# A linear-attention and GeGLU block on one core: later loads of x and Q's weights, and a down projection in pairs of row tiles

## The chip, the core and the metric

The kernel runs on one core of one Trainium2 chip. The metric is the device time in microseconds (us): 527.69 us is the median of 16 runs of the kernel before, from 526.3 to 528.41. The profile is of one execution of it, which took 526.3 us; its span, from the first to the last recorded instruction, is 524.6 us, and the remaining 1.7 us lie around it.

A core has five instruction streams that run beside each other: TensorE (PE in the profile, with its weight loads as PEld), VectorE (DVE), ScalarE (ACT), GpSimd (POOL) and SyncE (SP, which only issues transfers here).

## What is computed

```python
def reference(A_x, A_wqkv, A_wo, B_x, B_w_gate, B_w_up, B_w_down):
    def _A_ref(x, wqkv, wo):                     # S = 2048, D = 576, H = 32 heads of 18
        qkv = (x @ wqkv).reshape(B, S, 3, H, Dh)...
        q, k, v = qkv[0], qkv[1], qkv[2]
        phi = lambda t: jnp.where(t > 0, t + 1, jnp.exp(t)) + 1e-6
        pq, pk = phi(q), phi(k)
        kv = einsum("bhsd,bhse->bhde", pk, v)
        z = einsum("bhsd->bhd", pk)
        num = einsum("bhqd,bhde->bhqe", pq, kv)
        den = einsum("bhqd,bhd->bhq", pq, z)[..., None] + 1e-6
        return (num / den)... @ wo
    def _B_ref(x, w_gate, w_up, w_down):         # F = 4608
        return (_gelu(x @ w_gate) * (x @ w_up)) @ w_down
    xn = _layernorm(A_x)
    return A_x + _A_ref(xn, A_wqkv, A_wo) + _B_ref(xn, B_w_gate, B_w_up, B_w_down)
```

All tensors are bf16. `B_x` isn't used.

## The kernel before

**Tiles and stages.** The 2048 tokens are 16 tiles of 128, and 4 chunks (`sc`) of 512. The first 68.6 us of the span are the attention's first half: layer norm of each tile, its transpose `xnT`, K for each tile (`k_half`, line 249), the accumulation of the product of phi(K) and the normalized x (`g_accumulate`, line 293), and Q for each chunk and each of five chunks of heads (`q_unit`, line 346; 126 rows for four of them, 72 for the fifth). From these come `zrep` and `kvT`, one block-diagonal matrix for each chunk of heads. Then, for each chunk of tokens, `gu_pair` runs 18 times (gate and up projection, two blocks of 128 columns each), and `down_tile` four times.

**Row tiles.** `gu_pair` doesn't use the 128 x 128 array as one piece. The class `_Unit` (line 306) gives its upper 64 rows (`LO`) and lower 64 rows (`HI`) a matmul each, which run beside each other and write two different banks of PSUM. In `p1` LO writes bank 0 and HI bank 1; in `p2` they change places, so that both banks hold full sums. Between the two a relay stands: an empty instruction on another engine's queue waits for the last matmul of `p1`, and the first matmul of `p2` waits for it. The relay is on POOL's queue for all blocks of `gu_pair` but the first, which uses SP's. PSUM has 8 banks, and the ring `banks` (line 304) hands them out in order.

**The down projection.** `down_tile` (line 664) uses the whole array: for each half of the 576 output columns, 36 matmuls of 128 rows against the hidden layer `hT` (line 677) and 5 against the scaled phi(Q) `pqT` and `m_sb` (line 682), all into one bank. At the start of chunk 0's first half, `m_stage` makes `m_sb`, the product of `kvT` and the output weights, with two matmuls each (line 659) and two ScalarE copies (line 662) before f = 0, 6, 12, 18 and 24. In the halves after it the hook `dn` makes the next chunk's denominators, one chunk of heads in each half of a tile: one matmul of 512 columns (`den_mm`, line 455), its eviction on VectorE (`den_evac`, line 449), four reciprocals of 128 columns on VectorE (line 479), and one multiplication of `pqT` on POOL (line 482). Chunk 0's denominators, and those of the fifth chunk of heads for chunk 1, are made inside `gu_pair`. There the multiplication on POOL is issued one block of `gu_pair` after its reciprocals.

**Order.** The schedule is written out by hand: the list `todo` holds the attention's first half, each step with a number by which the list is sorted, and every engine executes its instructions in the order in which the program issues them. The loads stand at the top: x's tiles on SP's queue, K's weights (`load_w(1)`) on ACT's queue.

Of the kernel before, what the change touches and what calls it, by code (L numbers as in the profile page):

```python
# [9 lines left out]
ALU = mybir.AluOpType  # L10
BF16 = mybir.dt.bfloat16
# [16 lines left out]
HALF = D // 2  # L28
KT = 5
HCH = [7, 7, 7, 7, 4]  # L30
HOFF = [0, 7, 14, 21, 28]
NCH = len(HCH)
CR = 7 * DH
# [23 lines left out]
def kernel(  # L57
# [11 lines left out]
    nc = tc.nc  # L69
# [5 lines left out]
    out_view = out.flatten_outer_dims().rearrange("(p n) d -> p n d", n=NS)  # L75
# [6 lines left out]
    fwork = ctx.enter_context(tc.tile_pool(name="fwork", bufs=3))  # L82
# [9 lines left out]
    def load_x(n0, cnt):  # L92
        nc.sync.dma_start(x_sb[:, n0:n0 + cnt, :], x_view[:, n0:n0 + cnt, :])
# [21 lines left out]
    load_x(0, 1)  # L115
    load_x(1, 1)
    load_x(2, 2)
    load_x(4, 4)
    load_w(0)
    load_x(8, 4)  # L120
    load_x(12, 4)

    nc.vector.memset(wqkv_sb[HP:P, 4, :], 0.0)
    nc.vector.memset(wqkv_sb[0:1, 0, D:D + 2], 0.0)
# [20 lines left out]
    zrep = persist.tile([P, NCH, CR], BF16, name="zrep")  # L145
    kvT = persist.tile([P, NCH, CR], BF16, name="kvT")

    nc.vector.memset(pqT[HP:P, NCH - 1, 0:2 * SC], 0.0)
    nc.vector.memset(zrep[HP:P, NCH - 1, :], 0.0)

    def load_wo():
        nc.sync.dma_start(wo2[:CR, 0:4, :], A_wo[0:4 * CR, :].rearrange("(c p) j -> p c j", p=CR))
# [153 lines left out]
    class _Unit:  # L306
# [12 lines left out]
                start=start, stop=stop, skip_group_check=True,  # L319
            )  # L320

        def p1(self):
            for kt in self.first:
                self.mm(0, LO, kt, kt == self.first[0], False)
                last = self.mm(1, HI, kt, kt == self.first[0], False)
            self.turn = self.relay.nop()
            tc.add_manual_dep(self.turn.ins, last.ins.name, SYNC, reason="the row tiles take turns on a bank")

        def p2(self):
            for kt in self.then:  # L330
                m = self.mm(1, LO, kt, False, kt == self.then[-1])
# [114 lines left out]
    def den_evac(sc, c, ps):  # L446
        rows = DH * HCH[c]
        d = dwork.tile([P, SC], F32, name="den_sb", tag="den_sb", bufs=6)
        nc.vector.tensor_scalar_add(out=d[:rows, :], in0=ps, scalar1=EPS_ATT)
        den_sb[sc, c] = d  # L450

    def den_mm(sc, c, bank):
        rows = DH * HCH[c]
        ps = ps_all[:rows, bank, :]
        nc.tensor.matmul(ps, lhsT=zrep[:rows, c, :rows], rhs=pqT[:rows, c, sc * SC:(sc + 1) * SC], start=True, stop=True)  # L455
        den_evac(sc, c, ps)

    def den_pair(items, outs):

        rows = DH * HCH[items[0][1]]  # L460

        def part(r):

            return slice(r.start, min(r.stop, P if rows <= P - HP + 8 else rows))

        return _Unit(
            outs,
            lambda i, r, kt: zrep[part(r), items[i][1], :rows],
            lambda i, r, kt: pqT[part(r), items[i][1], items[i][0] * SC:(items[i][0] + 1) * SC],
            nc.sync, first=(0,), then=(0,),  # L470
        )

    def den_norm(sc, c, q, pieces):
        w = SC // pieces
        rows = DH * HCH[c]
        d = den_sb[sc, c][:rows, q * w:(q + 1) * w]
        cols = slice(sc * SC + q * w, sc * SC + (q + 1) * w)
        for h in range(0, w, P):
            nc.vector.reciprocal(out=d[:, h:h + P], in_=d[:, h:h + P])  # L479

        def scale():
            nc.gpsimd.tensor_tensor(out=pqT[:rows, c, cols], in0=pqT[:rows, c, cols], in1=d, op=ALU.mult)  # L482
        return scale
# [48 lines left out]
        ]  # L532

    todo += [(t, spin, count) for t, count in [(5.80, 3), (6.20, 5), (8.50, 2)]]
    todo.sort(key=lambda x: x[0])

    tail = next(i for i, (_, step, n) in enumerate(todo) if step is STEPS[-1][0] and n == NS - 1) + 1
# [77 lines left out]
    def gu_pair(sc, k):  # L615
        cs = slice(sc * SC, (sc + 1) * SC)
        blk = sc * (NF // GUB) + k
        wg, wu, wr = gu_blocks.pop(blk)
        units = []
        for i in range(GUB):  # L620
            b = [banks.next(), banks.next()]
            fcol = slice(i * P, (i + 1) * P)

            def lhs(a, rows, kt, fcol=fcol):
                if kt == 4:
                    return wr[rows, fcol]
# [12 lines left out]
        den = None  # L639
        if sc == 0 and 0 <= k - DEN_FROM < len(DEN_PAIRS):  # L640
            items = DEN_PAIRS[k - DEN_FROM]
            den = den_pair(items, [ps_all[:DH * HCH[c], banks.next(), :] for _, c in items])
            den.p1()
        for i, (b, u) in enumerate(units):
            u.p2()
            gl = fwork.tile([P, SC], F32, name="gl")
            nc.scalar.activation(out=gl[:], in_=ps_all[:, b[0], :], func=ACT.Gelu_apprx_tanh)  # L647
            nc.vector.tensor_tensor(out=hT[:, GUB * k + i, :], in0=ps_all[:, b[1], :], in1=gl[:], op=ALU.mult)  # L648
        if den:
            den.p2()  # L650
            for (dsc, c), ps in zip(items, den.outs):
                den_evac(dsc, c, ps)

    def m_stage(c, acc_bank):
        rows = DH * HCH[c]
        for hf in range(2):
            b = (acc_bank + 2 + (2 * c + hf) % 6) % 8
            hs = slice(hf * HALF, (hf + 1) * HALF)
            nc.tensor.matmul(  # L659
                ps_all[:rows, b, :HALF], lhsT=kvT[:rows, c, :rows], rhs=wo2[:rows, c, hs], start=True, stop=True,  # L660
            )
            nc.scalar.copy(out=m_sb[:rows, c, hs], in_=ps_all[:rows, b, :HALF])

    def down_tile(sc, j, hooks):
        n = sc * TPC + j
        ts_ = slice(n * P, (n + 1) * P)
        res = fwork.tile([P, D], BF16, name="res")
        last = n == NS - 1
        for hf in range(2):
            hs = slice(hf * HALF, (hf + 1) * HALF)  # L670
            todo = hooks.pop(0) if hooks else {}
            acc_bank = banks.next()
            acc = ps_all[:, acc_bank, :HALF]
            for f in range(NF):
                if f in todo:
                    todo[f](acc_bank)
                nc.tensor.matmul(  # L677
                    acc, lhsT=hT[:, f, j * P:(j + 1) * P], rhs=wd_sb[:, f, hs], start=(f == 0), stop=False,
                )
            for c in range(NCH):  # L680
                rows = DH * HCH[c]
                nc.tensor.matmul(  # L682
                    acc, lhsT=pqT[:rows, c, ts_], rhs=m_sb[:rows, c, hs], start=False, stop=(c == NCH - 1),
                )
            nc.vector.tensor_tensor(out=res[:, hs], in0=acc, in1=x_sb[:, n, hs], op=ALU.add)  # L685
            if last:
                nc.sync.dma_start(out_view[:, n, hs], res[:, hs])
        if not last:
            nc.sync.dma_start(out_view[:, n, :], res[:])

    for sc in range(NSC):
        for k in range(NF // GUB):
            gu_pair(sc, k)
            if scales:
                scales.pop(0)()
            if den_jobs and k > DEN_FROM:
                scales.append(den_norm(*den_jobs.pop(0)))
        while wd_loaded[0] < NF:
            load_wd_slice()

        hooks = [{6 * c_: (lambda b, c_=c_: m_stage(c_, b)) for c_ in range(NCH)} if sc == 0 else {}]
        if sc + 1 < NSC:
            for c_ in range(NCH):
                def dn(b, c=c_, nsc=sc + 1):
                    if (nsc, c) not in den_sb:
                        den_mm(nsc, c, (b + 2) % 8)
                    den_norm(nsc, c, 0, 1)()
                hooks.append({0: dn})
        for j in range(TPC):
            down_tile(sc, j, hooks)  # L710


# [28 lines left out]
```

## Time and profile before

| | before |
|---|---|
| median of 16 runs | 527.69 us |
| profiled execution | 526.3 us |
| its span | 524.6 us |
| TensorE busy | 517.6 us, 99% of the span |
| first K matmul | at 9.25 us |
| end of the attention's first half | 68.6 us |
| gate and up, each of chunks 1 to 3 | 70.0 us |
| down projection, chunks 0 to 3 | 42.5, 41.4, 41.4 and 40.3 us |
| mean granted TensorE clock | 0.997 |

The columns of a group's line are: source line, engine, operation, output and inputs with their shapes, count, then busy time in us and mean duration in ns, and last the idle time of the engine just before. Matmuls overlap in the array, so the recorded 286 ns of a 288-column matmul isn't its share of the time; that share is the distance between starts, which the chain of waits shows as time over count. In that chain only the matmuls that carry it are counted: of a pair of row tiles one.

### The profile page before, as it was taken

The numbers are of one execution on the slowest core, as the hardware profiler recorded it, in microseconds if no ns is written. First come the engines' busy times: TensorE is split into PE (matmuls) and PEld (weight loads), VectorE is DVE, ScalarE is ACT, GpSimd is POOL, SyncE is SP. The second block draws the span as 40 slices with busy tenths as digits, with TensorE's granted clock in tenths as the row PEclk, the third lists the DMA queues.
The fourth block names the chain that finished last, engine by engine and source line by source line (L and its number), as shares of the span: only waits on it lengthen the run. The fifth ranks groups of instructions, "written<-read, shape, count | busy, mean of one in ns | idle before, by whom it ended". The sixth has DMA issues, their size and how long they took to land.

```text
span 524.6 us, 10640 instructions
## 1 busy us (share of the span) xinstructions
PE 517.6 (99%) x4498; PEld 315.2 (60%) x4498; DVE 250.6 (48%) x435; ACT 143.2 (27%) x293; POOL 35.1 (7%) x55
## 2 busy tenths in 40 slices
PE   6999999999999999999999999999999999999997
PEld 6777764555577754444577744444777544445775
DVE  5897574977348423333378133334485233333101
ACT  4999543223230012332200023233000123322000
POOL 2011100111002100000011000000021000000000
PEclk8999999999999999999999999999999999999999
DMA  8233809899600035555400055555100355540000
GB/s 280 56 55 62 221 1 238 252 269 264 180 26 24 12 101 150 156 150 157 114 13 12 23 162 157 155 156 145 44 24 13 102 151 159 145 136 2 12 11 24
DMA packets 106282, 57.89 MB, mean 110 GB/s; under 512 B 13370, under 2 KB 105722, under 8 KB 106234
## 3 DMA queue, kind: packets, MB, share of 16 engines
q1 hardware_dynamic: 105626, 56.55, 38.6%
q8 instruction: 35, 0.57, 0.4%
q10 hardware_dynamic: 608, 0.66, 0.4%
q14 instruction: 13, 0.11, 0.1%
HBM read 52.86 MB, written 2.36 MB: 105 GB/s over the span
## 4 chain that ended last, share of the span: by engine, by line
PE 98%; DMA 1%; ACT 0%; DVE 0%; issue 0%
PE ps_all L317 55%; PE ps_all L677 27%; PE ps_all L249 4%; PE ps_all L293 4%; PE ps_all L682 4%; PE ps_all L346 3%; DMA wqkv_sb<-in_A_wqkv_dram 1%; PE ps_all L455 1%; PE ps_all L437 0%; PE ps_all L659 0%; PE ps_all L235 0%; ACT L114 0%; DVE res L685 0%; PE ps_all L426 0%; PE ps_all L137 0%
## 5 line engine op out<-in xcount | busy, mean ns | idle before, releaser
L317 PE MATMUL ps_all<-xnT,wg 64*128 64x512 bf16 x1152 | 272.6, 376 | 0.0
L317 PE MATMUL ps_all<-xnT,wu 64*128 64x512 bf16 x1152 | 271.7, 376 | 0.0
L648 DVE TENSOR_TENSOR hT<-ps_all,gl 128x512 bf16<-128x512 f32 x144 | 99.4, 690 | 162.0 <-ACT gl L647 161.4
L647 ACT ACTIVATE gl<-ps_all 128x512 f32<-128x512 f32 x144 | 86.0, 597 | 314.4 <-PE ps_all L317 295.0
L317 PEld LDWEIGHTS <-wu 64*128 64x128 bf16 x1152 | 108.3, 94 | 66.3
L317 PEld LDWEIGHTS <-wg 64*128 64x128 bf16 x1152 | 108.3, 94 | 66.1
L677 PE MATMUL ps_all<-wd_sb,hT 128*128 128x288 bf16 x1152 | 147.0, 286 | 0.0
L677 PEld LDWEIGHTS <-hT 128*128 128x128 bf16 x1152 | 112.3, 98 | 30.6 <-issue 1.3
L479 DVE RECIPROCAL den_sb<-den_sb 126x128 f32<-126x128 f32 (+1 forms) x80 | 68.3, 910 | 0.5
L685 DVE TENSOR_TENSOR res<-ps_all,x_sb 128x288 bf16<-128x288 f32 x32 | 14.6, 457 | 88.0 <-PE ps_all L682 88.0
L317 PE MATMUL ps_all<-xnT,wr 64*128 64x512 bf16 x288 | 55.1, 376 | 0.0
L482 POOL TENSOR_TENSOR pqT<-pqT,den_sb 126x512 bf16<-126x512 bf16 (+3 forms) x25 | 24.1, 965 | 317.3 <-DVE den_sb L479 282.7
L249 PE MATMUL ps_all<-wqkv_sb,xnT 128*128 128x288 bf16 x160 | 23.5, 295 | 2.6 <-DMA wqkv_sb<-in_A_wqkv_dram 2.6
L682 PE MATMUL ps_all<-m_sb,pqT 126*128 126x288 bf16 (+1 forms) x160 | 24.9, 285 | 0.0
L317 PEld LDWEIGHTS <-wr 64*128 64x128 bf16 x288 | 14.5, 94 | 16.8 <-issue 0.7
L293 PE MATMUL ps_all<-hT,xn 128*128 128x288 bf16 (+4 forms) x176 | 22.4, 275 | 0.0
L249 PEld LDWEIGHTS <-xnT 128*128 128x128 bf16 x160 | 15.9, 101 | 8.5 <-issue 2.8
L293 PEld LDWEIGHTS <-xn 128*128 128x128 bf16 (+1 forms) x176 | 17.5, 102 | 4.1
L682 PEld LDWEIGHTS <-pqT 126*128 126x128 bf16 (+1 forms) x160 | 15.5, 97 | 4.1
L346 PE MATMUL ps_all<-xnT,wqkv_sb 128*126 128x512 bf16 (+1 forms) x70 | 17.4, 378 | 0.0
L277 DVE SCALAR_TENSOR_TENSOR hT<-ps_all,phi_e 128x288 bf16<-128x288 f32 x32 | 13.2, 448 | 7.6 <-ACT phi_e L273 7.4
L269 ACT ACTIVATE phi_e<-ps_all 128x288 f32<-128x288 f32 x32 | 12.9, 408 | 6.0 <-PE ps_all L249 4.6
(67 smaller groups left out, 176.0 us busy)
## 6 DMA issues: line engine op xcount, KB each, us to landing
wg<-in_B_w_gate_dram SPq DMA_DIRECT2D x72, 256.0 KB, 2.9
wu<-in_B_w_up_dram SPq DMA_DIRECT2D x72, 256.0 KB, 3.6
wd_sb<-in_B_w_down_dram SPq DMA_DIRECT2D x12, 432.0 KB, 4.7
wr<-in_B_w_gate_dram SPq DMA_DIRECT2D x72, 32.0 KB, 2.8
wr<-in_B_w_up_dram SPq DMA_DIRECT2D x72, 32.0 KB, 3.1
out_dram<-res SPq DMA_DIRECT2D x15, 144.0 KB, 1.8
x_sb<-in_A_x_dram SPq DMA_DIRECT2D x3, 576.0 KB, 8.3
wqkv_sb<-in_A_wqkv_dram SPq DMA_DIRECT2D x2, 576.0 KB, 4.7
```

Source lines behind the costliest of these rows:

```text
L249: nc.tensor.matmul(ps_all[:, k_bank(n, hf), :HALF], lhsT=xnT[:, kt, n * P:(n + 1) * P], rhs=wqkv_sb[:, kt, D + hf * HALF:D + (hf + 1) * HALF],
L277: nc.vector.scalar_tensor_tensor(out=out_, in0=ps, scalar=0.0, in1=e, op0=ALU.max, op1=ALU.add)
L293: nc.tensor.matmul(ps_all[:m, b, col:col + w], lhsT=xn[:, n, j0:j0 + m], rhs=pk[:, n, d0:d0 + w], start=(n == 0 and col == 0), stop=(n == ...
L317: return nc.tensor.matmul(self.outs[i], lhsT=self.lhs(i, rows, kt), rhs=self.rhs(i, rows, kt), start=start, stop=stop, skip_group_check=True,)
L346: nc.tensor.matmul(ps, lhsT=wqkv_sb[:, kt, q0:q0 + rows], rhs=xnT[:, kt, sc * SC:(sc + 1) * SC], start=(kt == 0), stop=(kt == KT - 1),)
L479: nc.vector.reciprocal(out=d[:, h:h + P], in_=d[:, h:h + P])
L482: nc.gpsimd.tensor_tensor(out=pqT[:rows, c, cols], in0=pqT[:rows, c, cols], in1=d, op=ALU.mult)
L647: nc.scalar.activation(out=gl[:], in_=ps_all[:, b[0], :], func=ACT.Gelu_apprx_tanh)
L648: nc.vector.tensor_tensor(out=hT[:, GUB * k + i, :], in0=ps_all[:, b[1], :], in1=gl[:], op=ALU.mult)
L677: nc.tensor.matmul(acc, lhsT=hT[:, f, j * P:(j + 1) * P], rhs=wd_sb[:, f, hs], start=(f == 0), stop=False,)
L682: nc.tensor.matmul(acc, lhsT=pqT[:rows, c, ts_], rhs=m_sb[:rows, c, hs], start=False, stop=(c == NCH - 1),)
L685: nc.vector.tensor_tensor(out=res[:, hs], in0=acc, in1=x_sb[:, n, hs], op=ALU.add)
```

## The change

The loads of x from tile 4 on, and of Q's weights, leave the top of the program. They become entries of `todo` with numbers 5.0 to 5.03, which is behind the statistics of tiles 0 and 1. The first entry is a VectorE memset of one element of tile 4, and the load of tile 4 waits for it; the other loads are behind that one on SP's queue.

The second half of the fifth chunk of heads is filled with zeros in more tensors: `pqT` over all tokens instead of half of them, and `kvT`, `m_sb` and `wo2` besides `zrep`. These memsets are on VectorE, ahead of the first statistics.

The down projection, the products for `m_sb` and the next chunk's denominators are computed in `_Unit`s, as gate and up are; only the last tile of tokens keeps the whole array. A unit of the down projection is one tile of 128 tokens with both halves of the columns: 41 pairs of row tiles in `p1`, 41 in `p2`. The order is p1 of tile 0, then for each next tile its p1 and the p2 of the one before. The relays are on ACT's queue. `m_sb`'s units are inside tile 0's p1 of chunk 0, the denominators' units inside tile 1's p1, two chunks of heads in one unit. When a denominators' unit has ended, its two evictions and up to eight reciprocals are issued in a row. All denominators' units of a chunk use the same pair of banks, `p[3]`.

```diff
     load_x(0, 1)
     load_x(1, 1)
     load_x(2, 2)
-    load_x(4, 4)
-    load_w(0)
-    load_x(8, 4)
-    load_x(12, 4)
...
-    nc.vector.memset(pqT[HP:P, NCH - 1, 0:2 * SC], 0.0)
-    nc.vector.memset(zrep[HP:P, NCH - 1, :], 0.0)
+    nc.vector.memset(pqT[HP:P, NCH - 1, :], 0.0)
+    for t in (zrep, kvT, m_sb, wo2):
+        nc.vector.memset(t[HP:P, NCH - 1, :], 0.0)
...
+    todo += [(5.0, lambda n: nc.vector.memset(x_sb[0:1, n, 0:2], 0.0), 4)]
+    todo += [(5.01, lambda n: load_x(n, 4), 4), (5.02, lambda n: load_w(0), 0)]
+    todo += [(5.03, lambda n: load_x(n, 4), n) for n in (8, 12)]
...
-    def m_stage(c, acc_bank):
...
+    def m_unit(c, b):
+        rows = DH * HCH[c]
+        return _Unit(
+            [ps_all[:rows, b + i, :HALF] for i in range(2)],
+            lambda i, r, kt: kvT[part(r, c), c, :rows],
+            lambda i, r, kt: wo2[part(r, c), c, i * HALF:(i + 1) * HALF],
+            nc.scalar, first=(0,), then=(0,),
+        )
...
+    def down_unit(n, b):
...
+        steps = range(NF + NCH)
+        return _Unit([ps_all[:, b + i, :HALF] for i in range(2)], lhs, rhs, nc.scalar, steps, steps)
...
+    def run_turns(step, units, first, gap, done):
+
+        hooks = {}
+        for i, u in enumerate(units):
+            hooks[first + step * i] = u.p1
+
+            def end(u=u, i=i):
+                u.p2()
+                done(i, u)
+            hooks[first + step * i + gap] = end
+        return hooks
+
+    def down(sc):
+
+        p = [banks.tiles[(banks.i + 2 * k) % 8] for k in range(4)]
+        n0 = sc * TPC
+        last = sc == NSC - 1
+        u = [down_unit(n0 + j, p[j % 3]) for j in range(TPC - last)]
+        hooks = [{}, {}]
+        if sc == 0:
+            ms = [m_unit(c, p[3 - c % 2]) for c in range(NCH)]
+            hooks[0] = run_turns(6, ms, 9, 3, m_copy)
+        if not last:
+            items = [[(sc + 1, 0), (sc + 1, 1)], [(sc + 1, 2), (sc + 1, 3)]]
+            if (sc + 1, NCH - 1) not in den_sb:
+                items.append([(sc + 1, NCH - 1), (sc + 2, NCH - 1)])
+            dens = [den_pair(it, [ps_all[:DH * HCH[c], p[3] + i, :] for i, (_, c) in enumerate(it)], nc.scalar) for it in items]
+
+            def den_out(k, unit):
+                for (dsc, c), ps in zip(items[k], unit.outs):
+                    den_evac(dsc, c, ps)
+                for dsc, c in items[k]:
+                    if dsc == sc + 1:
+                        den_norm(dsc, c, 0, 1)()
+            hooks[1] = run_turns(12, dens, 4, 3, den_out)
+        u[0].p1(hooks[0])
+        for j in range(1, len(u)):
+            u[j].p1(hooks[1] if j == 1 else ())
+            u[j - 1].p2()
+            down_out(n0 + j - 1, u[j - 1].outs)
+        u[-1].p2()
+        down_out(n0 + len(u) - 1, u[-1].outs)
+        if last:
+            down_last(NS - 1, p[0])
+        elif (sc + 1, NCH - 1) in den_sb and len(items) == 2:
+            den_norm(sc + 1, NCH - 1, 0, 1)()
+        banks.i += 2
```

`m_copy` is the two ScalarE copies that `m_stage` had. `down_out` adds x to both halves of a tile on VectorE and stores it; `down_last` is `down_tile`'s body for the last tile. `p1` and `p2` take hooks: a function to be called before a given step. `gu_pair` itself is unchanged but for the relay that it now names (`nc.sync`) for chunk 0's denominators.

More of the change, by code (lines that the diff above doesn't have):

```diff
@@ L320, in mm, with p1 @@
             )
-        def p1(self):
+        def p1(self, hooks=()):
             for kt in self.first:
+                if kt in hooks:
+                    hooks[kt]()
                 self.mm(0, LO, kt, kt == self.first[0], False)
@@ L327, in p1, with p2 @@
             tc.add_manual_dep(self.turn.ins, last.ins.name, SYNC, reason="the row tiles take turns on a bank")
-        def p2(self):
+        def p2(self, hooks=()):
             for kt in self.then:
+                if kt in hooks:
+                    hooks[kt]()
                 m = self.mm(1, LO, kt, False, kt == self.then[-1])
@@ L450, in den_evac, with part, den_pair @@
         den_sb[sc, c] = d
[L452 to L458, printed above, removed]
+    def part(r, c):
+        return slice(r.start, P if c == NCH - 1 else CR) if r is HI else r
+    def den_pair(items, outs, relay):
         rows = DH * HCH[items[0][1]]
-        def part(r):
-            return slice(r.start, min(r.stop, P if rows <= P - HP + 8 else rows))
         return _Unit(
             outs,
-            lambda i, r, kt: zrep[part(r), items[i][1], :rows],
-            lambda i, r, kt: pqT[part(r), items[i][1], items[i][0] * SC:(items[i][0] + 1) * SC],
-            nc.sync, first=(0,), then=(0,),
+            lambda i, r, kt: zrep[part(r, items[i][1]), items[i][1], :rows],
+            lambda i, r, kt: pqT[part(r, items[i][1]), items[i][1], items[i][0] * SC:(items[i][0] + 1) * SC],
+            relay, first=(0,), then=(0,),
         )
@@ L641, in gu_pair @@
             items = DEN_PAIRS[k - DEN_FROM]
-            den = den_pair(items, [ps_all[:DH * HCH[c], banks.next(), :] for _, c in items])
+            den = den_pair(items, [ps_all[:DH * HCH[c], banks.next(), :] for _, c in items], nc.sync)
             den.p1()
@@ L652, in gu_pair, with m_copy @@
                 den_evac(dsc, c, ps)
-    def m_stage(c, acc_bank):
+    def m_unit(c, b):
[6 more added lines that the diff above has]
+        )
+    def m_copy(c, u):
         rows = DH * HCH[c]
         for hf in range(2):
-            b = (acc_bank + 2 + (2 * c + hf) % 6) % 8
-            hs = slice(hf * HALF, (hf + 1) * HALF)
[L659 to L662, printed above, removed]
@@ L664, in down_tile, with lhs, rhs @@
-    def down_tile(sc, j, hooks):
-        n = sc * TPC + j
+            nc.scalar.copy(out=m_sb[:rows, c, hf * HALF:(hf + 1) * HALF], in_=u.outs[hf])
+    def down_unit(n, b):
+        sc, j = divmod(n, TPC)
+        ts_ = slice(n * P, (n + 1) * P)
+        def lhs(i, r, kt):
+            return hT[r, kt, j * P:(j + 1) * P] if kt < NF else pqT[part(r, kt - NF), kt - NF, ts_]
+        def rhs(i, r, kt):
+            hs = slice(i * HALF, (i + 1) * HALF)
+            return wd_sb[r, kt, hs] if kt < NF else m_sb[part(r, kt - NF), kt - NF, hs]
+        steps = range(NF + NCH)
+        return _Unit([ps_all[:, b + i, :HALF] for i in range(2)], lhs, rhs, nc.scalar, steps, steps)
@@ L666, in down_tile, with down_out, down_last @@
+    def down_out(n, outs):
+        res = fwork.tile([P, D], BF16, name="res")
+        for hf in range(2):
+            hs = slice(hf * HALF, (hf + 1) * HALF)
+            nc.vector.tensor_tensor(out=res[:, hs], in0=outs[hf], in1=x_sb[:, n, hs], op=ALU.add)
+        nc.sync.dma_start(out_view[:, n, :], res[:])
+    def down_last(n, b):
         ts_ = slice(n * P, (n + 1) * P)
         res = fwork.tile([P, D], BF16, name="res")
-        last = n == NS - 1
         for hf in range(2):
             hs = slice(hf * HALF, (hf + 1) * HALF)
-            todo = hooks.pop(0) if hooks else {}
-            acc_bank = banks.next()
-            acc = ps_all[:, acc_bank, :HALF]
+            acc = ps_all[:, b + hf, :HALF]
@@ L674, in down_tile @@
             for f in range(NF):
-                if f in todo:
-                    todo[f](acc_bank)
                 nc.tensor.matmul(
-                    acc, lhsT=hT[:, f, j * P:(j + 1) * P], rhs=wd_sb[:, f, hs], start=(f == 0), stop=False,
-                )
+                    acc, lhsT=hT[:, f, (n % TPC) * P:(n % TPC + 1) * P], rhs=wd_sb[:, f, hs], start=(f == 0), stop=False)
             for c in range(NCH):
@@ L682, in down_tile @@
                 nc.tensor.matmul(
-                    acc, lhsT=pqT[:rows, c, ts_], rhs=m_sb[:rows, c, hs], start=False, stop=(c == NCH - 1),
-                )
+                    acc, lhsT=pqT[:rows, c, ts_], rhs=m_sb[:rows, c, hs], start=False, stop=(c == NCH - 1))
             nc.vector.tensor_tensor(out=res[:, hs], in0=acc, in1=x_sb[:, n, hs], op=ALU.add)
-            if last:
-                nc.sync.dma_start(out_view[:, n, hs], res[:, hs])
-        if not last:
-            nc.sync.dma_start(out_view[:, n, :], res[:])
+            nc.sync.dma_start(out_view[:, n, hs], res[:, hs])
@@ L699 @@
             load_wd_slice()
[L701 to L710, printed above, removed]
+        down(sc)
 _INS = ['A_x', 'A_wqkv', 'A_wo', 'B_x', 'B_w_gate', 'B_w_up', 'B_w_down']
```

## The prediction

> **What bounds the kernel now.** I read the page's busy shares and its chain of waits first, then the chain in order of time, then the timeline at the joints that the change touches, then the start in slices of 1 us.
>
> ```profile
> PE 517.6 (99%) x4498; PEld 315.2 (60%) x4498; DVE 250.6 (48%) x435; ACT 143.2 (27%) x293; POOL 35.1 (7%) x55
> PE 98%; DMA 1%; ACT 0%; DVE 0%; issue 0%
> L479 DVE RECIPROCAL den_sb<-den_sb 126x128 f32<-126x128 f32 (+1 forms) x80 | 68.3, 910 | 0.5
> ```
>
> TensorE sets the end from 9.25 us on. Busy shares could hide gaps, so I take the cadence from the chain in order of time (start, duration, what):
>
> ```profile
> 1.95 7.25 DMA wqkv_sb<-in_A_wqkv_dram
> 9.25 1.21 PE ps_all L249 x5
> ...
> 67.21 1.42 PE ps_all L437 x25
> ...
> 145.85 0.39 PE ps_all L659 x2
> ...
> 188.33 70.03 PE ps_all L317 x648
> 258.37 4.52 PE ps_all L677 x36
> 262.88 0.61 PE ps_all L682 x5
> 263.50 0.22 PE ps_all L455
> 263.72 4.41 PE ps_all L677 x36
> ```
>
> A 288-column matmul of the whole array costs 4.41 / 36 = 0.1225 us, a pair of 512-column row tiles 70.03 / 324 = 0.216 us. In both the columns per us are the same (2351 and 2370), so the array streams without gaps, and row tiles are no faster for the same rows. The first stretch after a change of mode is longer, 4.52 against 4.41. The timeline gives the durations behind the joints:
>
> ```profile
> 145.88 0.60 ACT L647 ACTIVATE gl<-ps_all 128x512 f32<-128x512 f32 x1 [0.27 <-PE ps_all L317]
> 146.51 0.69 DVE L648 TENSOR_TENSOR hT<-ps_all,gl 128x512 bf16<-128x512 f32 x1 [0.17 <-ACT gl L647]
> 152.67 0.68 DVE L449 TENSOR_SCALAR den_sb<-ps_all 126x512 f32<-126x512 f32 x1
> 153.39 3.39 DVE L479 RECIPROCAL den_sb<-den_sb 126x128 f32<-126x128 f32 x4
> 173.66 3.37 DVE L479 RECIPROCAL den_sb<-den_sb 72x128 f32<-72x128 f32 x4
> 177.11 1.16 POOL L482 TENSOR_TENSOR pqT<-pqT,den_sb 72x512 bf16<-72x512 bf16 x1 [3.29 <-DVE den_sb L479]
> ```
>
> And the start, in slices (busy time and counts, then clock, share of the DMA engines, GB/s):
>
> ```profile
> 8.00:9.00 1.00, 0.00 (x0) 0.00 (x0) 0.36 (x2) 0.00 (x0) 0.24 (x1) 1.00 1.09 311
> 9.00:10.00 1.00, 0.75 (x4) 0.49 (x4) 0.00 (x0) 0.00 (x0) 0.00 (x0) 0.72 1.17 322
> 10.00:11.00 1.00, 1.00 (x8) 0.83 (x7) 0.00 (x0) 0.41 (x1) 0.00 (x0) 0.50 1.04 256
> ```
>
> TensorE waits for K's weights here, with the DMA engines full, and then runs 3.4 us at half clock.
>
> **What the Trainium skill says.** "TensorEngine Tiling (Array Packing)", Key Properties: a change of tiling mode drains TensorE; the 0.11 us above agree. "TensorE: Matmul & The Clock Gate", Architectural detail: ACT and DVE execute strictly in order, GpSimd in order on each of its cores, and of TensorE's stream only weight loads are pulled ahead. The trace agrees as far as it goes: no eviction of line 449 overtakes the reciprocals ahead of it. The same page, Part 1: the clock gate judges free-running windows of 3413 ns; here TensorE stood still from 6.6 to 9.25 us and had half clock for one such window.
>
> **The change, part by part.**
>
> *Start.* The added zeros lengthen VectorE's work ahead of the first statistics: pqT doubles (0.48 us more), kvT 0.11 as zrep's, and m_sb and wo2 with 64x288 words each 0.27 (a third of the 0.78 that 64x864 took), 1.14 in all. VectorE was at 2.65 us then and waited until 3.15 for x, so statistics start at 3.79, 0.64 later; with the new one-element memset (0.06) tile 0's xnT, complete at 6.75 before, is complete at 7.45. K's weights: ahead of them are now x's tiles 0 to 3, together 1254 KB, which by the slices' GB/s had passed at 6.2 us. V's weights, of the same size and alone, land 4.7 us after issue, which gives 6.65. So the first K matmul is at 7.45, 1.8 us earlier. TensorE then stands still for 0.4 us, not 2.6, and may keep its clock, worth up to 1.7 us. But ACT is 97 to 100% busy from 11 to 17 us in most slices, so TensorE can't run far ahead. I take a gain of 2.2, between 3.5 and a loss of 0.5: x's tile 4 is issued at 5.9 and needed about 10.7; a load of 576 KB alone lands 4.7 later, in time, but one that took the crowded start's 8.3 would be late. Q's weights (12.7 by the GB/s) come before their first use at about 14.1.
>
> *Mode.* Seven changes between gate/up and down go, at about 0.1 each; one comes before the last tile: a gain of 0.6 (0.2 to 0.7).
>
> *The down projection itself.* A tile is 82 pairs of 288 columns for 82 whole matmuls: 0.1225 each, no change. Four instructions must then be issued in 0.1225 us; the chain's line 437 shows two in 1.42 / 25 = 0.057, so it fits. A 64-row weight load takes 94 ns and is hidden in 122. I take 0, bound 5 ns a pair above, 1230 pairs (15 tiles), 6 us. Below nothing it can't be, the columns bind.
>
> *m_sb, chunk 0.* Let t be 0 at tile 0's p1, and a step 0.1225. The first m unit stands at step 9, t = 1.10, but its banks are those of the last gate/up unit, which VectorE leaves at 1.52 (the 146.51 line, with t = 0 at 145.68): 0.47 wait. After that each unit's relay is on ACT behind the two copies of the unit before (0.77 for the two, 0.36 after the matmul's start, 0.08 for the relay), a cycle of 1.21 where the matmuls need 0.98: 4 x 0.23. The last copies start 0.36 after p2 and end 0.77 later, and step 40 reads them 4 steps and a pair after p2: 0.57. Sum 2.0. Before, these copies had 12 steps of cover.
>
> *Denominators, chunks 0 to 2.* In tile 1's p1, unit 0 is issued at step 4 and 7, its matmuls end at 1.47, the evictions at 2.20 and 2.88, then eight reciprocals keep VectorE until 9.7. Unit 1 at step 16 (2.39) needs the second eviction: 0.55, three times, 1.65. Chunk 1 has a third unit, at 4.84, in the same banks. Unit 1's evictions are behind the eight reciprocals and end at 11.1; TensorE stops until 11.15: 6.3. The kernel before had one denominator in each half tile, 4.1 us of VectorE in 5.25.
>
> *The tail of chunks 0 and 2.* The fifth chunk of heads' reciprocals are issued behind the last tile's output, so they start 1.1 after the down projection's end, end at 4.5, and POOL's multiplication at 5.75. Behind it on POOL's queue are the relays of the next gate/up units. TensorE does p1 of both units (2.16) and then waits for the first relay until 5.85: 3.7 each, 7.4. (Chunk 1 computes it inside the third unit.) VectorE's output additions of tile 0 are behind all reciprocals too, but end at 18.8 (chunk 0), before tile 3 takes the bank at 21.5.
>
> *Clock.* Stops of 6.3 and 3.7 us invite half clock for a window afterwards: 1.7 us lost each time. By the start's example I take 2.0 for the long one, 1.0 for each short one, 4.0 (0 to 7).
>
> Sum: 2.0 + 1.65 + 6.3 + 7.4 + 4.0 - 2.2 - 0.6 = +18.5 us on the profiled 526.3, 544.8. That execution was 1.4 below the median of 527.69; for the median I forecast 546.2.
>
> **Rivals.** *Issue of the row tiles binds.* The page on TensorE, Back-to-back issue gap, prices a weight load and matmul in a sustained stream at 81 ns; a pair then needs 162 instead of 122.5: 1230 x 0.0395 = 48.6, 594.8. For it: line 437's 57 ns were shown over 25 matmuls only. Against: gate/up has no gap at all, and 57 is below the page's figure.
>
> *The tail is hidden.* If POOL's relays don't stand behind the multiplication, 7.4 and 2.0 of clock go: 536.8. Against: the program issues the multiplication ahead of the next relay, and POOL has one queue. For it: POOL is busy 7% only, and where its relays stood before, no wait on them shows.
>
> *The waits on VectorE's queue don't reach TensorE: not slower.* One mechanism: the eight reciprocals are done before the third unit and the relays need VectorE and POOL. Then 6.3, 7.4, 1.65 and 4.0 go, and with the start at its upper 3.5 the sum is -2.2, 525.5. It decides when these waits total under 2.2 us; at the 3.39 us for four reciprocals there are 6.8 in the one place and 3.4 in the other, which the steps between (1.3 and 2.16) don't cover.
>
> **How the numbers follow.** Forecast 0.85, issue 0.07, hidden tail 0.05, not slower 0.03 (half of it faster). From the bounds the forecast's own sum runs from +11.6 to +32 if all fell together; the clock, the pair's price and the start make 536.5 to 557 likely, which takes in the hidden tail. This measurement can tell about 0.2%, 1.05 us, from no change: faster 0.015, same 0.015, slower 0.97.
>
> **What would show it.** In the changed profile: the first K matmul near 7.5 us and no half clock after it; matmuls of the down projection every 0.12 us; in chunk 1's down a stop of TensorE of 6 us behind line 450's eviction; after chunks 0 and 2 a stop of 3.7 us about 2.2 us into gate/up, but none after chunk 1; half clock after the stops. The forecast is wrong if pairs take over 0.13 us, or if these stops are absent.

## The result and the profile after

The changed kernel takes 539.89 us (median of 8 runs, 539.1 to 541.45) against 527.14 for the kernel before in the same comparison: 1.0242 times as long, with a 95% interval from 1.0231 to 1.0253, or 12.75 us more. The profiled execution took 539.51 us with a span of 537.8, 13.2 more than the span before. One execution each of the first run of experiment 1 and the last of experiment 2 was disturbed (1411.9 and 620.91 us), and their medians and ratios leave it out.

```profile
PE 522.5 (97%) x5752; PEld 344.8 (64%) x5752; DVE 248.5 (46%) x439; ACT 143.2 (27%) x293; POOL 35.1 (7%) x55
PEclk9999999999999999999979999999999899999999
PE 80%; issue 9%; DVE 8%; ACT 1%; DMA 1%; POOL 0%; DVEq 0%; POOLq 0%
```

These are the page's busy shares, clock row and chain of waits. TensorE's share of the chain fell from 98% to 80%, and VectorE has 8%; TensorE's own busy time grew by only 4.9 us, so most of the loss is waiting. The clock row has two dips inside the run. The places follow from cutting both traces at the first matmul of each stage:

| Stage | before | after | difference |
|---|---|---|---|
| attention's first half and Q, to the first gate/up matmul | 74.44 | 71.68 | -2.77 |
| gate/up, chunk 0, to the first down matmul | 71.63 | 71.22 | -0.41 |
| down, chunk 0 | 42.19 | 43.72 | +1.53 |
| gate/up, chunk 1 | 70.03 | 72.30 | +2.26 |
| down, chunk 1 | 41.42 | 49.77 | +8.35 |
| gate/up, chunk 2 | 70.04 | 69.93 | -0.11 |
| down, chunk 2 | 41.42 | 41.73 | +0.31 |
| gate/up, chunk 3 | 70.04 | 73.98 | +3.94 |
| down, chunk 3, to the last matmul | 40.11 | 40.19 | +0.08 |

(Before, the first two matmuls for `m_sb`, 0.30 us, stand ahead of the first down matmul and are counted in the row above it. Chunk 0's down projection therefore lost 1.23.)

**Start.** The chain in order of time, of the changed kernel (start, duration, what):

```profile
7.09 0.28 PE ps_all L133 x5
7.37 0.65 PE ps_all L246 x5
...
12.95 4.15 DMA xnT<-xn
17.10 0.05 issue
17.14 1.40 PE ps_all L246 x10
```

K's weights are no longer in the chain. The first K matmul is recorded at 7.21 us instead of 9.25; the chain counts the first five from the end of the work before them, 7.37, and they take 0.65 us instead of 1.21: they have the full clock. The first DMA transpose takes 4.15 us and sets when the fifth tile's K begins.

**The stop in chunk 1.** Timeline around the third denominators' unit:

```profile
266.72 6.62 DVE L474 RECIPROCAL den_sb<-den_sb 126x128 f32<-126x128 f32 x8
...
267.60 1.32 PE L314 MATMUL ps_all<-wd_sb,hT 64*128 64x288 bf16 x18
...
273.26 1.22 DVE L450 TENSOR_SCALAR den_sb<-ps_all 126x512 f32<-126x512 f32 x2
...
273.94 1.18 PE L314 MATMUL ps_all<-pqT,zrep 64*72 64x512 bf16 x2 [5.02 <-DVE den_sb L450]
```

TensorE has done the nine steps that lie between the second unit and the third at 268.7. The third unit's banks still hold the second unit's sums, whose evictions are behind eight reciprocals and start at 273.26. The bracket names them: 5.02 us idle, released by the eviction.

**The stop after chunk 0.** The same view, at the beginning of gate/up of chunk 1:

```profile
187.65 3.37 DVE L474 RECIPROCAL den_sb<-den_sb 72x128 f32<-72x128 f32 x4
...
188.65 0.38 PE L314 MATMUL ps_all<-xnT,wu 64*128 64x512 bf16 x1
191.10 1.16 POOL L477 TENSOR_TENSOR pqT<-pqT,den_sb 72x512 bf16<-72x512 bf16 x1 [22.65 <-DVE den_sb L474]
191.13 0.39 PE L314 MATMUL ps_all<-xnT,wu 64*128 64x512 bf16 x1 [2.11 <-POOLq L325]
```

The releaser is POOL's queue at line 325, the relay. TensorE starts 0.03 us after POOL's multiplication has begun, not after it has ended; experiment 5 looks into that. The same stop, also 2.11 us, stands at 422.5 us, after chunk 2.

**The clock.** The windows view, cut where the clock may change (length, busy time of PE, PEld, DVE, ACT and POOL with counts, granted clock, DMA share, GB/s):

```profile
186.88:190.29 3.41, 2.15 (x20) 1.43 (x16) 3.38 (x6) 0.00 (x0) 0.00 (x0) 1.00 0.34 102
190.29:193.71 3.42, 2.58 (x24) 1.19 (x26) 1.42 (x2) 1.17 (x2) 1.16 (x1) 1.00 0.40 114
...
268.81:272.23 3.42, 0.11 (x2) 0.00 (x0) 3.42 (x5) 0.00 (x0) 1.16 (x1) 1.00 0.01 2
272.23:275.64 3.41, 1.69 (x10) 0.95 (x11) 3.41 (x6) 0.00 (x0) 1.16 (x1) 0.50 0.00 0
275.64:279.05 3.41, 3.41 (x31) 3.09 (x29) 3.41 (x5) 0.00 (x0) 1.13 (x1) 0.50 0.00 0
...
422.41:425.83 3.42, 1.31 (x14) 0.50 (x12) 2.33 (x3) 0.00 (x0) 1.01 (x1) 1.00 0.71 201
425.83:429.24 3.41, 3.41 (x20) 1.20 (x16) 1.38 (x2) 1.19 (x2) 0.14 (x1) 0.50 0.12 31
```

After a window with little work the next has half clock: 0.11 of 3.42 us before 272.23, 1.69 before 275.64, 1.31 before 425.83. The stop after chunk 0 is as long as the one after chunk 2, but it lies across the joint of two windows, which keep 2.15 and 2.58 us of work, and nothing follows. That is the difference between the 2.26 us lost in gate/up of chunk 1 and the 3.94 of chunk 3.

### The profile page after: what moved, and what is told of

It is laid out like the page before. It is cut to its first block, busy times and chain, and to the rows that moved or that the text cites. A ratio compares the mean times of both kernels' runs of the same rounds, so it can differ in the third digit from the quotient of the medians.

```text
span 537.8 us, 13167 instructions
## 1 busy us (share of the span) xinstructions
PE 522.5 (97%) x5752; PEld 344.8 (64%) x5752; DVE 248.5 (46%) x439; ACT 143.2 (27%) x293; POOL 35.1 (7%) x55
## 4 chain that ended last, share of the span: by engine, by line
PE 80%; issue 9%; DVE 8%; ACT 1%; DMA 1%; POOL 0%; DVEq 0%; POOLq 0%
PE ps_all L314 69%; DVE den_sb L474 6%; PE ps_all L290 4%; PE ps_all L246 3%; PE ps_all L347 2%; PE ps_all L698 2%; DVE den_sb L450 1%; DMA xnT<-xn 1%; POOL pqT L477 0%; DVE stats L208 0%; PE ps_all L438 0%; ACT xnT L235 0%; PE ps_all L702 0%; ACT phi_e L270 0%; DVE pqT L144 0%
## 5 line engine op out<-in xcount | busy, mean ns | idle before, releaser
L314 PE MATMUL ps_all<-wd_sb,hT 64*128 64x288 bf16 x2160 | 146.7, 284 | 0.0
L314 PEld LDWEIGHTS <-hT 64*128 64x128 bf16 x2160 | 130.7, 95 | 10.0 <-issue 2.5
L314 PE MATMUL ps_all<-xnT,wr 64*128 64x512 bf16 x288 | 63.7, 378 | 0.0
L687 DVE TENSOR_TENSOR res<-ps_all,x_sb 128x288 bf16<-128x288 f32 x30 | 12.1, 445 | 83.3 <-PE ps_all L314 83.3
L314 PEld LDWEIGHTS <-wr 64*128 64x128 bf16 x288 | 18.2, 95 | 16.1 <-issue 0.6
L314 PE MATMUL ps_all<-m_sb,pqT 64*128 64x288 bf16 (+1 forms) x300 | 27.4, 288 | 0.0
L314 PEld LDWEIGHTS <-pqT 64*128 64x128 bf16 (+1 forms) x300 | 20.0, 95 | 1.0 <-issue 0.2
L450 DVE TENSOR_SCALAR den_sb<-ps_all 126x512 f32<-126x512 f32 (+1 forms) x20 | 12.6, 669 | 17.4 <-PE ps_all L314 17.4
L314 PE MATMUL ps_all<-pqT,zrep 64*126 64x512 bf16 (+2 forms) x40 | 11.1, 405 | 5.6 <-DVE den_sb L450 5.4
```

The lines of the kernel that those rows point to most:

```text
L314: return nc.tensor.matmul(self.outs[i], lhsT=self.lhs(i, rows, kt), rhs=self.rhs(i, rows, kt), start=start, stop=stop, skip_group_check=True,)
L687: nc.vector.tensor_tensor(out=res[:, hs], in0=outs[hf], in1=x_sb[:, n, hs], op=ALU.add)
```

## The experiments

Spans are of profiled executions (before 524.6, changed 537.8), times are medians, and each ratio is to the kernel before in the same comparison.

**1. The later loads alone**, in two runs. The edit is the change's first and last hunk on the kernel before:

```diff
     load_x(2, 2)
-    load_x(4, 4)
-    load_w(0)
-    load_x(8, 4)
-    load_x(12, 4)
...
+    todo += [(5.0, lambda n: nc.vector.memset(x_sb[0:1, n, 0:2], 0.0), 4)]
+    todo += [(5.01, lambda n: load_x(n, 4), 4), (5.02, lambda n: load_w(0), 0)]
+    todo += [(5.03, lambda n: load_x(n, 4), n) for n in (8, 12)]
```

> The kernel before with the later loads alone, without the added zeros and with the old down projection. If the start's gain stands by itself, the first K matmul comes at 6.8 to 7.4 us, the half clock after it goes, the attention's first half ends 2.8 to 3.4 us earlier than 68.6, and the span is 521.1 to 521.9 us (before 524.6). Rival: the later loads only help with the rest of the change, or delay x's later tiles; then the span stays at 524.6 or above.

523.98 us, 0.9932 (0.9905 to 0.9959). The second run gives the profile:

> The later loads alone again, for a profile that can be read: first K matmul at 6.8 to 7.2 us, no half clock behind it, the attention's first half 2.8 to 3.4 us shorter, span 521 to 522.

523.63 us, 0.9939 (0.9927 to 0.9952); span 521.6. Its chain in order of time:

```profile
1.95 5.33 DMA wqkv_sb<-in_A_wqkv_dram
7.28 0.04 issue
7.32 0.79 PE ps_all L245 x5
```

K's weights landed 5.3 us after issue instead of 7.25, and the clock didn't fall. The first K matmul is at 7.32, later than the 6.8 to 7.2 expected: without the zeros, the transfer is still what it waits for. All stages from the first gate/up matmul on are within 0.03 us of before. The first part of the change is a gain of 3.3 us by itself (526.94 for the kernel before in this comparison, less 523.63).

**2. The down projection alone, with the old loads.**

> The changed kernel with the loads back at the top of the program. If the two parts add up, it loses the 2.8 us of the start and perhaps 0.6 more, because the added zeros then lie ahead of nothing that waits for weights: span 540.4 to 541.2 (changed kernel 537.8). Rival: the loads gain nothing of their own and the whole difference is in the down projection; then 537.8.

545.39 us, 1.0344 (1.0316 to 1.0372); span 542.7. The stages from the first gate/up matmul on are as in the changed kernel, within 0.15 us. But the start is 4.7 us longer than in the changed kernel, and 2.0 longer than before: K's weights land at 10.72 us. The sum of the two parts doesn't come out, and neither the expectation nor its rival has this span; 1.4 to 2 us more are lost here than the loads gain on the old kernel. Two runs look for them in the added zeros. The first has the zeros alone on the kernel before:

```diff
-    nc.vector.memset(pqT[HP:P, NCH - 1, 0:2 * SC], 0.0)
-    nc.vector.memset(zrep[HP:P, NCH - 1, :], 0.0)
+    nc.vector.memset(pqT[HP:P, NCH - 1, :], 0.0)
+    for t in (zrep, kvT, m_sb, wo2):
+        nc.vector.memset(t[HP:P, NCH - 1, :], 0.0)
```

> The kernel before with the added zeros alone, loads and down projection as they were. K's weights set the first K matmul there (9.25 us) and the transposes are ready 2.6 us earlier, so 1.2 us more on VectorE should stay hidden: span 524.6. Rival, from the run with the old loads and the new down projection, whose first K matmul came at 10.76 and whose attention was 2 us later than before: the zeros, or what they delay, move the transfers; then 526 to 527.

527.64 us, 1.001 (0.9999 to 1.002); span 525.7. The median moves by 0.2% at most. The profile isn't as expected, though: its first K matmul is at 9.64 us, its fifth, which waits for a second, smaller load of K's weights, at 10.40, and the span is 1.1 us longer than before, between the expectation and the rival. One execution can't tell that from chance. The second has the new down projection, the old loads and the zeros of `kvT`, `m_sb`, `wo2` and of `pqT`'s second half moved to POOL:

> The new down projection with the old loads, and the added zeros on POOL instead of VectorE. With the zeros on VectorE this pairing had its first K matmul at 10.76 us and lost 4.7 us to the changed kernel, though the later loads alone gain 3.3. If the zeros ahead of the statistics are the other 1.4 to 2, the first K matmul comes back to 9.3 and the span to 540.7 to 541.3. Rival: the weights land late for another reason, and 542.7 stays.

545.56 us, 1.034 (1.0292 to 1.0389); span 543.8. The start is as long with the zeros on POOL as with them on VectorE (76.37 and 76.40 us to the first gate/up matmul), so VectorE's zeros aren't what the new down projection with the old loads loses here. Its chain shows K's weights again, at 9.94 us:

```profile
1.96 7.98 DMA wqkv_sb<-in_A_wqkv_dram
9.99 1.36 PE ps_all L252 x5
```

TensorE stood still longer than before, and two windows had half clock instead of one, up to 15.1 us. Why the first K matmul comes anywhere from 9.25 to 10.76 us with the same loads, and whether the new program has the late end of it by more than chance, stays open; there is one profile of each kernel.

**3. The fifth chunk of heads a tile earlier**, after tile 1's output instead of after the last tile's:

```diff
             down_out(n0 + j - 1, u[j - 1].outs)
+            if j == 2 and not last and len(items) == 2:
+                den_norm(sc + 1, NCH - 1, 0, 1)()
...
-        elif (sc + 1, NCH - 1) in den_sb and len(items) == 2:
-            den_norm(sc + 1, NCH - 1, 0, 1)()
```

> The changed kernel with the fifth chunk of heads' reciprocals and multiplication of chunks 0 and 2 issued a tile earlier, when VectorE is idle. If the stops at the start of gate and up come from POOL's queue behind these reciprocals, both go, and with them the half clock after the second: gate and up of chunk 1 from 72.3 to 70.0, of chunk 3 from 74.0 to 70.0, span 531.6. Rival: the stops belong to the change from one kind of work to the other (banks, ScalarE's first activation); then they stay and the span is 537.8.

532.96 us, 1.0106 (1.0082 to 1.0131); span 531.4. Gate/up of chunks 1 and 3 takes 69.93 us each, and there is no half clock in it. Both stops are gone, at the time expected.

**4. Only POOL's multiplication later**, the reciprocals where they were:

```diff
         elif (sc + 1, NCH - 1) in den_sb and len(items) == 2:
-            den_norm(sc + 1, NCH - 1, 0, 1)()
+            scales.append(den_norm(sc + 1, NCH - 1, 0, 1))
```

> The changed kernel with the same reciprocals in the same place, but POOL's multiplication behind them issued one block of gate and up later. If the relay on POOL's queue is what stops TensorE, this is as good as moving the reciprocals: span 531.6. Rival: VectorE, busy with the reciprocals for 3.4 us, is what gate and up wait for; then the stops stay, at 537.8.

533.3 us, 1.0112 (1.0087 to 1.0136); span 532.1, gate/up again 69.93 each. VectorE is as busy as before at the joint:

```profile
188.56 3.37 DVE L474 RECIPROCAL den_sb<-den_sb 72x128 f32<-72x128 f32 x4
191.86 1.23 DVE L647 TENSOR_TENSOR hT<-ps_all,gl 128x512 bf16<-128x512 f32 x2
```

The first multiplication for the hidden layer is held behind the reciprocals, and TensorE doesn't notice. What stopped it was the relay's place on POOL's queue alone.

**5. What a relay waits for.** Four memsets of an unused tile behind the late multiplication:

```diff
             den_norm(sc + 1, NCH - 1, 0, 1)()
+            for _ in range(4):
+                nc.gpsimd.memset(scr[:], 0.0)
```

> The changed kernel with four memsets of 128x512 float32 issued on POOL behind the late multiplication of chunks 0 and 2, which depend on nothing that is late. In the changed profile TensorE starts again at 191.13 us, when POOL's multiplication has just begun (191.10), not when it has ended. If a relay passes as soon as the work ahead of it on its queue has been issued, the memsets add under 0.5 us to each stop, and the span stays within 1 us of 537.8. Rival: the relay waits for work ahead of it to end (or for room in the queue); then each stop grows by the memsets' time, 1 us or more each, span 540 or above.

547.99 us, 1.0394 (1.0362 to 1.0426); span 544.8. Timeline after chunk 0:

```profile
191.01 1.16 POOL L478 TENSOR_TENSOR pqT<-pqT,den_sb 72x512 bf16<-72x512 bf16 x1 [22.65 <-DVE den_sb L475]
192.11 2.27 POOL L755 MEMSET scr<- 128x512 f32 x4
193.91 0.60 PE L315 MATMUL ps_all<-xnT,wu 64*128 64x512 bf16 x1 [4.97 <-POOLq L326]
```

The memsets were expected to add under 0.5 us, and the stop grew by 2.86 (2.11 to 4.97). The span is in the rival's range, but the rival, in its plain form, falls too. The four memsets last 525 ns each and fill 2.27 us, so they start 0.58 apart and the last begins at 193.86 and ends at 194.38; TensorE starts at 193.91. The trace has the relay itself, at 193.84: after the end of the third memset (193.80) and just ahead of the start of the fourth. So a relay goes together with the last instruction ahead of it, and that instruction has waited for the end of the one before it. In the changed kernel, where the multiplication is the last, the relay's record stands at 191.06, ahead of the multiplication's start (191.10), and its 1.16 us aren't waited for. The longer stops cost the clock after both chunks.

**6. Evictions ahead of all reciprocals.** The reciprocals of all units are issued after the last unit's evictions:

```diff
-                for dsc, c in items[k]:
-                    if dsc == sc + 1:
-                        den_norm(dsc, c, 0, 1)()
+                if k == len(items) - 1:
+                    for dsc, c in sum(items, []):
+                        if dsc == sc + 1:
+                            den_norm(dsc, c, 0, 1)()
```

> The changed kernel with the evictions of all denominators' units issued ahead of any reciprocal. If the eight reciprocals between unit 1's matmuls and its evictions are what stops TensorE in chunk 1, the stop of 5 us and the half clock of 6.8 us behind it go: chunk 1's down projection from 49.9 to 41.8, span 529.6. Then the sum of the additions of the third tile's bank must still hold: VectorE's reciprocals end later than before in tile 1, but before tile 3. Rival: the third unit waits for its own operands (POOL's multiplication, the relay on ScalarE) and keeps 3 us or more of the stop: 533 or above.

535.91 us, 1.0153 (1.0119 to 1.0186); span 534.2, with chunk 1's down projection at 46.3 us. The span is in the rival's range, but not for the rival's reason. The stop at the third unit is gone, and another has come, which cost the clock too. It is plainest in the run with this order and that of experiment 3 together:

> Both new orders together: evictions ahead of reciprocals, and the fifth chunk of heads a tile earlier. If the three stops and the clock behind them are the whole loss, span 537.8 - 8.1 - 6.4 = 523.3, below the kernel before (524.6) by about what the start gains less 1.2 for the wait for the first product for m_sb's banks. Rival: row tiles in the down projection cost something of their own that the stops hide; then 526 or above.

529.36 us, 1.0035 (1.0022 to 1.0047); span 526.2, chunk 1's down projection 44.75. Of the sixteen executions eight have a mean granted clock of 1.0 and take 527.94 to 529.09 us, the profiled one among them; the other eight have 0.997, as one window of 3.41 us at half clock gives, and take 529.62 to 530.8. Its timeline, two tiles later:

```profile
269.18 16.36 DVE L474 RECIPROCAL den_sb<-den_sb 126x128 f32<-126x128 f32 x20
...
285.45 1.48 DVE L687 TENSOR_TENSOR res<-ps_all,x_sb 128x288 bf16<-128x288 f32 x4
...
285.90 4.93 PE L314 MATMUL ps_all<-wd_sb,hT 64*128 64x288 bf16 x72 [1.72 <-DVE res L687]
```

Twenty reciprocals now stand ahead of tile 0's output addition, and tile 3's accumulation needs that bank. Of the 2.9 us still missing to the expected span this stop has 2.0 with its restart, and chunk 1's two short waits of a unit for the eviction of the unit before have 0.7, 0.2 idle in the record and 0.35 of lost cadence each. So the span is in the rival's range as well, but hardly anything is left for a cost of the row tiles themselves.

**7. Filling the stop.** 80 matmuls on constants ahead of the third unit, which leave nothing in the output:

```diff
+                def filled():
+                    for _ in range(80):
+                        nc.tensor.matmul(ps_all[:, p[2], 0:P], lhsT=ident[:], rhs=ident[:], start=True, stop=True)
+                    third()
```

> The changed kernel with 80 matmuls of 128 columns on constants, into banks that nobody uses then, ahead of the third denominators' unit of chunk 1, where TensorE stands still for 5.2 us. They take 80 x 0.056 = 4.5 us, inside the stop. If half clock comes from the stop's idle time, the two windows at half clock (272.2 to 279.1) become one or none, and up to 2.5 us come back: span 535.3. Rival: the half clock has another cause, and the matmuls cost nothing and gain nothing: 537.8; or the stop isn't idle, and they are added: 542.

537.18 us, 1.0185 (1.0149 to 1.022); span 536.3. From 260 to 290 us the clock is full, and chunk 1's down projection takes 47.69 instead of 49.77. So 2.1 of its 8.35 us were the clock's. The span gains only 1.5, since the start was 0.7 longer in this execution (72.38 against 71.68). And in this run the stop after chunk 0 met the windows badly (73.98 in gate/up) and the one after chunk 2 well (72.29), the reverse of the changed kernel.

**8. All orders mended.** These are the main lines; the reciprocals' two old places go too, and zeros and loads change as the expectation says:

```diff
-            ms = [m_unit(c, p[3 - c % 2]) for c in range(NCH)]
-            hooks[0] = run_turns(6, ms, 9, 3, m_copy)
+            ms = [m_unit(c, p[2 + c % 2]) for c in range(NCH)]
+            hooks[0] = run_turns(6, ms, 7, 3, m_copy)
...
-            dens = [den_pair(it, [ps_all[:DH * HCH[c], p[3] + i, :] ...
+            dens = [den_pair(it, [ps_all[:DH * HCH[c], p[3 - k % 2] + i, :] ...
...
+            if j == 1 and not last:
+                for c in (0, 1):
+                    den_norm(sc + 1, c, 0, 1)()
             u[j - 1].p2()
             down_out(n0 + j - 1, u[j - 1].outs)
+            if j < 3 and not last:
+                for c in ((2, 3), (4,))[j - 1]:
+                    den_norm(sc + 1, c, 0, 1)()
```

> The changed kernel with its orders mended: evictions ahead of all reciprocals, the reciprocals dealt out between the tiles' output additions, denominators' units in two pairs of banks by turns, the units for m_sb two steps earlier and beginning with the other pair of banks, the added zeros on POOL, x's last four tiles behind the first DMA transpose. If the waits named so far are all there is, down projections of 42.3, 41.5 and 41.1 us, gate and up of 69.9, span 519.5 to 521. Rival: the row tiles' down projection brings nothing over the old one, and the later loads alone are as good, 521.8.

523.13 us, 0.9929 (0.9917 to 0.9941); span 522.0. It beats both kernels, by 16.8 us the changed one. The down projections take 42.48, 41.52, 41.09 and 40.28 us, gate/up of chunks 1 to 3 69.93 each. No line of its waits has TensorE waiting for VectorE's evictions or POOL's queue. The span is 1 to 2.5 us above the expectation; the start has 0.8 of it (72.30 to the first gate/up matmul, where the later loads alone have 71.49). That is no more than the start varies by itself: from 71.59 to 72.38 in the seven kernels here that share the changed kernel's. So whether x's last four tiles behind the transpose bring anything isn't shown. Against the later loads alone (0.9939, 0.9927 to 0.9952) the difference can't be told from none. From the first gate/up matmul to the last of all, its stages add up to 446.4 us and those of the loads alone to 446.9: row tiles in the down projection are worth half a microsecond in these two profiles.

## Why the prediction was right, and where its sizes were off

It forecast 546.2, slower, with a range from 536.5 to 557; 539.89 is slower and inside. Its long stops stand where it put them, and no others do; of the short waits, those that it put behind ScalarE's copies didn't come. The sum was 18.5 us where the spans differ by 13.2. By its own steps:

- **Start**: forecast -2.2, measured -2.8 (-2.1 to -2.9 over the seven kernels with this start). The first K matmul was forecast at 7.45 and came at 7.21; the clock held. The bound set for late tiles of x wasn't needed.
- **Mode and the down projection's pace**: forecast -0.6 and 0. Chunk 3, the only down projection without units inside, went from 40.11 to 40.19. Each of the gate/up stages without a stop is 0.11 us shorter, and the mended kernel's 0.5 us from gate/up on is of this term's size. The rival that four instructions can't be issued in 0.1225 us is refuted: 40.19 us are 328 steps of 0.1225, 246 of them pairs of row tiles and 82 the last tile's whole matmuls.
- **m_sb and chunk 0's denominators**: forecast 2.55, measured 1.23. The failed term is the 4 x 0.23 for relays behind ScalarE's copies. The timeline:

```profile
144.49 0.28 PE L314 MATMUL ps_all<-wo,kvT 62*126 62x288 bf16 x1 [0.20 <-DVE hT L647]
...
145.30 0.70 ACT L667 CAST m_sb<-ps_all 126x288 bf16<-126x288 f32 x2 [1.59 <-PE ps_all L314]
...
145.41 0.34 PE L314 MATMUL ps_all<-wo,kvT 64*126 64x288 bf16 x2
...
145.91 0.35 PE L314 MATMUL ps_all<-wo,kvT 64*126 64x288 bf16 x2
```

  The second unit's p2 is at 145.91, 0.50 after its p1 and on the steps' cadence, while the copies ahead of its relay run until 146.00. The relay's record stands at 145.80: as on POOL, it doesn't wait for the end of the copy ahead. The first unit's wait for the last gate/up unit's bank was there (144.49, on VectorE's line 647), at 0.37 of lost cadence against 0.47, and the ten matmuls that read the last copies took 1.28 us instead of 0.86, 0.42 against 0.57.
- **Denominators, chunk 1, with the clock**: forecast 0.55 + 6.3 + 2.0, measured 8.35. TensorE went on 0.05 us after the first of the two evictions had ended (273.89 to 273.94), where the sum had it wait for the second, and the stop cost 5.2 us (5.3 from start to start, less a step) instead of 6.3. Chunk 2's 0.55 was 0.31.
- **The tail**: forecast 3.7 each, stops of 2.1 idle and about 2.3 of lost time each. The step that failed is "ends at 5.75": the relay was put behind the end of POOL's multiplication. The reciprocals ended 4.4 us after the down projection, as forecast, and TensorE was released 0.03 us after the multiplication had begun. The term is 2.8 too large over both stops; the rival of a hidden tail is refuted by experiments 3 and 4.
- **Clock**: forecast 4.0, measured about 2.1 in chunk 1 (experiment 7) and 1.7 in chunk 3 (3.94 less 2.26), nothing after chunk 0. The size is right in part by luck: the sum put 1.0 on each of the two equal stops, and 1.7 fell on one of them and nothing on the other, as the windows happened to lie.

The waits on VectorE's queue did reach TensorE, so the rival that ended on the other side is refuted too.

The mechanism was right, then, and the main error of size is one assumption used twice: that a relay on another engine's queue waits for the end of the work ahead of it. It overstates the tail by 2.8 us and the products for `m_sb` by 0.9, which is 3.7 of the 5.3 us between sum and measurement.

## What to carry to other kernels

When instructions are bundled, ask of each in-order queue what is now behind what. Here two chunks of heads per unit put eight reciprocals ahead of an eviction, and one multiplication ahead of the relays of the next stage, and the costs came out later, on an engine that had got no more work. Evict first, deal the long work out between what others wait for, and count again after each mending, since moving one stop away made another. A change of two parts deserves a run of each: here the start was worth 3.3 us by itself, and the other part hid it.

## What the runs showed that was not expected

An empty instruction that hands a semaphore on doesn't wait for the end of the instruction ahead of it on its engine. On POOL its record stands 0.02 to 0.04 us ahead of the start of that instruction (191.06 and 191.10 in the changed kernel, 193.84 and 193.86 in experiment 5), and TensorE follows 0.07 later (191.13, 193.91). The instruction further ahead had ended (the third memset at 193.80).

The clock changes at joints 3.41 us apart (272.23 and 425.83 are 45 such steps apart), and these don't move with the work: 2.15 us of matmuls in a window kept the full clock and 1.31 lost it for the next, so that a stop of 2.1 us left the clock alone in one place and cost it 1.7 us in another. Over all the profiles here, the most recorded work in a window at full clock that lost it is 1.60 us (experiment 6's first run, from 285.83), and the least that kept it is 1.83 (experiment 2's first run, from 191.92). In a window at half clock, where the same matmuls take longer, 1.99 us weren't enough to end it (the same run, from 277.25). The Trainium skill, "TensorE: Matmul & The Clock Gate", Part 1, describes free-running windows of this length and agrees; its table has half clock after an idle window, while here a window with 1.60 us of work was followed by it.
